# Column halves throughout the second expert layer, and earlier combine weights, in an attention and soft mixture-of-experts kernel

## The chip, the cores and the metric

The kernel runs on one core of a Trainium2 chip. The metric is the device time of one execution in microseconds (us). The core's engines are written as in the profile: PE is TensorE (its matmuls; PEld its weight loads), DVE is VectorE, ACT is ScalarE, POOL is GpSimd, SP is SyncE, which here issues every data transfer. Each engine works through its own queue in order.

## The reference

Attention with 32 pooled keys per head comes first, and its output, 4608 rows of 512, goes into a soft mixture of 8 experts with 4 slots each:

```python
logits = x @ phi                                   # 4608 x 32
d = exp(logits - logits.max(0)); d /= d.sum(0)     # over the rows
slot_input = (d.T @ x).reshape(8, 4, 512)
for e in range(8):
    h = maximum(slot_input[e] @ w1[e], 0)          # 4 x 1024
    slot_out[e] = h @ w2[e]                        # 4 x 512
c = exp(logits - logits.max(1)); c /= c.sum(1)     # over the slots
out = c @ slot_out.reshape(32, 512)                # 4608 x 512
```

Everything is float32. `w1` and `w2` are 16 MB each, the output is 9.4 MB.

## The kernel before, in words

**Stages.** The batches are taken in four pairs: keys and values are pooled, scores and softmax formed, logits made, and each pair's share of the slot inputs summed. The shares are joined into `SIM` (line 1000), the slot inputs of all experts, which holds each expert's 4 slots in columns of their own and zeros beside them. Then three things follow. The first layer (`expert_in`, line 1097) multiplies `SIM` with `w1`, two tiles of 1 MB per expert; `hidden` (lines 1113, 1122 and 1128) applies the rectifier and transposes the result into `hT`, four experts at a time. The second layer (`expert_out`, line 1148) multiplies `hT` with `w2`, again two tiles of 1 MB per expert, 16 in all. The output stage (`out_mult`, line 1280) multiplies the combine weights `cT` with the slot outputs `sr`, 36 row blocks of 128 x 512, copies each from a PSUM bank to SBUF on ACT or DVE and writes it out.

**The second layer.** One tile of `w2` takes four matmuls of 32 columns of weights each, which stand side by side in the array and write the four quarters of the 128 partitions. All tiles of all experts add into one accumulator, since the unused rows of `hT` are zero. So at the end the accumulator holds, in each quarter of the partitions, a part of the sum for all 32 slots; a matmul with `rep` (line 1080), a matrix of four stacked identities repeated, adds the four quarters and repeats the result. The accumulator `pacc` is the PSUM tile `kvbank`, two banks of 512 floats. Before the change the first 15 tiles add 512 columns wide into bank 0. The last tile (expert 7, second half) comes in four transfers of 256 KB, two for each half of the columns, and its products are made apart: the first column half goes to bank 1, the second to the first half of bank 0.

**`slot_sums` (lines 1070, 1075 and 1080).** It copies an accumulator from PSUM to SBUF, the first column half on DVE and the second on ACT, and multiplies it with `rep` into `scbank`, one bank for each half. It is called twice: `slot_sums(0)` for the first 15 tiles, ahead of the last tile's products, and `slot_sums(1)` for the last tile; the two matmuls for a half add up in `scbank`. After it, line 1266 on ACT rounds each half of the sum to `sr` and line 1271 on DVE stores the rounding's remainder beside it; the output matmuls use both (two matmuls per block).

**Combine weights.** `slots(bp)` makes `cT` for one of the four pairs: about nine DVE instructions of 0.2 to 0.5 us (lines 1198 to 1220), one exponential on ACT, five transposes on PE into two banks (line 1231) and three copies on ACT (lines 1240 to 1244). Before the change it stands behind every second expert of the second layer.

**Fills.** `fill` adds matmuls of ones into an unused half bank of `kvbank` (line 476) that nothing reads. Two stand behind the 15th `w2` tile.

**What sets the order.** Each piece of work is handed to a planner (`add`) with its engine, an estimated cost and what it reads and writes. The planner picks, step by step, the piece that can start first by its own clock (ties by the order of the program) and so fixes the order in each engine's queue before anything runs; the costs and the place in the program move work only that way. The waits between engines are put in afterwards by the framework, from the tiles that are read and written. It takes `kvbank` and `scbank` as wholes: an access to one bank waits for the other engines' earlier accesses to the other bank.

**The end.** The first output tile of three row blocks is written in three transfers of 256 KB (line 1313) so that it can start early; its six half blocks are copied at lines 1302 (ACT) and 1304 (DVE), alternating. The other 33 blocks go in 11 transfers of 768 KB (line 1343), with copies at lines 1333 (ACT) and 1335 (DVE).

## Time and profile before

| | |
|---|---|
| Time, median of three runs | 216.18 us (216.16 to 221.99) |
| Profiled execution, its own time | 219.04 us |
| Its span, first to last instruction | 217.2 us |
| Busy in the span | PE 175.2, PEld 108.8, DVE 131.7, ACT 70.0, POOL 86.6 us |
| Moved by DMA | 76.45 MB, mean 352 GB/s |
| Granted PE clock, mean | 0.918 |

A row of the timeline gives start, length, engine, line, operation and form, the count, and in brackets how long the engine had been idle and for what. A float32 matmul stands in the trace as two records, so the four matmuls of a `w2` tile are "x8". The chain of waits follows the work that ended last back to the start, each piece to what released it; "issue" in it is time in which the engine waited for nothing that the profile shows. In a table of stretches each engine has its busy time and, in brackets, its instructions; then come the granted PE clock as a fraction, the busy share of the 16 DMA engines, and what they moved.

### The profile page before, as it was taken

Reading aid. Unit: us, or ns where it says so; the run is one execution under the profiler, and the core shown is the slowest. Engines: PE = TensorE matmul, PEld = TensorE weight load, DVE = VectorE, ACT = ScalarE, POOL = GpSimd, SP = SyncE. Lnnn points to the kernel's source line nnn. Section 1 sums busy time; section 2 is a strip of 40 time slices with the busy share of each in tenths; the row PEclk is TensorE's granted clock in tenths of the full one; section 3 lists DMA queues with packets and bytes.
Section 4 is the critical chain, followed back from the end, with each engine's and each line's share of the span. In section 5 each row is a group of like instructions: output and inputs, shape, how many; then the busy total and the mean of one; then the engine's idle time right before and its main releaser. Section 6 shows DMA issues by size and latency. Waiting matters only on the chain.

```text
span 217.2 us, 5728 instructions
## 1 busy us (share of the span) xinstructions
PE 175.2 (81%) x2462; PEld 108.8 (50%) x2462; DVE 131.7 (61%) x226; ACT 70.0 (32%) x186; POOL 86.6 (40%) x85
## 2 busy tenths in 40 slices
PE   8798977696598997969889799777999995899600
PEld 6576754465474574455565368543553331366200
DVE  6835047969539999967964995459300750189600
ACT  2042234443423726134742332020100321267500
POOL 6298009697952795399932484200000000000000
PEclk9999999859579999799997999996999999999955
DMA  6999999999999999999889979499999995059997
GB/s 214 386 392 391 380 393 375 390 381 392 385 388 389 385 408 347 393 391 388 322 293 414 367 269 400 118 410 345 409 404 410 408 407 195 5 199 416 414 413 295
DMA packets 28985, 76.45 MB, mean 352 GB/s; under 512 B 1824, under 2 KB 6944, under 8 KB 28960
## 3 DMA queue, kind: packets, MB, share of 16 engines
q1 hardware_dynamic: 28960, 76.09, 92.8%
q8 instruction: 19, 0.31, 0.6%
q14 instruction: 6, 0.05, 0.1%
HBM read 66.65 MB, written 9.44 MB: 350 GB/s over the span
## 4 chain that ended last, share of the span: by engine, by line
PE 40%; DMA 22%; DVE 13%; POOL 9%; issue 6%; ACT 3%; SPq 1%; DVEq 1%; POOLq 0%; ACTq 0%
DMA top<-in_q_dram 10%; DMA arena<-in_moe_w_dram 9%; PE kvbank L476 7%; PE bank L1097 6%; PE bank L785 5%; PE scbank L716 5%; PE kvbank L599 4%; PE bank L1280 3%; DMA out_dram<-arena 3%; DVE arena L700 3%; POOL arena L562 3%; POOL arena L774 3%; PE bank L849 2%; POOL arena L751 2%; DVE arena L511 2%
## 5 line engine op out<-in xcount | busy, mean ns | idle before, releaser
L549 POOL TENSOR_TENSOR arena<-arena 128x1152 f32<-128x1152 f32 x8 | 21.0, 2631 | 17.4 <-ACT arena L544 14.7
L476 PE MATMUL kvbank<-ones 128*128 128x256 f32 x96 | 26.2, 411 | 2.2 <-ACT arena L622 1.1
L700 DVE STREAM_TRANSPOSE arena<-top 128x1152 f32<-128x1152 f32 x16 | 21.7, 1358 | 7.0 <-DMA top<-in_q_dram 7.0
L716 PE MATMUL scbank<-arena 64*64 64x288 f32 x256 | 22.5, 447 | 3.0 <-DVE arena L730 2.5
L774 POOL TENSOR_TENSOR arena<-arena,ssm 128x576 f32<-128x576 f32 x16 | 18.4, 1158 | 15.6 <-DVE ssm L770 15.6
L562 POOL TENSOR_TENSOR arena<-arena 128x128 f32<-128x128 f32 (+2 forms) x32 | 23.4, 730 | 2.3 <-ACT arena L555 0.3
L599 PE MATMUL kvbank<-arena 64*32 64x128 f32 x1152 | 20.7, 278 | 4.3 <-ACT arena L555 2.7
L785 PE MATMUL bank<-arena 128*128 128x288 f32 x64 | 21.8, 475 | 2.0 <-DVE arena L777 2.0
L751 POOL TENSOR_TENSOR arena<-arena,smx 128x576 f32<-128x576 f32 x16 | 18.4, 1158 | 12.3 <-DVE smx L746 12.3
L476 PEld LDWEIGHTS kvbank<-ones 128*128 128x128 f32 x96 | 18.2, 202 | 7.7 <-issue 2.5
L599 PEld LDWEIGHTS kvbank<-arena 64*32 64x32 f32 x1152 | 16.5, 107 | 8.4 <-issue 3.8
L511 DVE TENSOR_REDUCE arena<-arena 128x128 f32<-128x1152 f32 x8 | 17.1, 2143 | 5.1 <-DMA arena<-in_phi_dram 5.1
L1148 PE MATMUL kvbank<-arena 128*32 128x512 f32 (+1 forms) x136 | 15.6, 573 | 3.8 <-DMA arena<-in_moe_w_dram 2.6
L730 DVE STREAM_TRANSPOSE arena<-scbank 128x576 f32<-128x576 f32 x16 | 12.2, 764 | 9.2 <-PE scbank L716 9.1
L785 PEld LDWEIGHTS bank<-arena 128*128 128x128 f32 x64 | 12.7, 215 | 7.5 <-DVE arena L777 3.0
L777 DVE STREAM_TRANSPOSE arena<-arena 128x576 f32<-128x576 f32 x16 | 12.2, 760 | 5.2 <-POOL arena L774 5.0
L1097 PE MATMUL bank<-arena,SIM 128*32 128x256 f32 x224 | 13.9, 409 | 1.7 <-DVE SIM L1000 1.7
L1280 PE MATMUL bank<-sr,cT 64*128 64x512 f32 (+1 forms) x78 | 14.6, 417 | 0.4 <-DVE sr L1271 0.2
L716 PEld LDWEIGHTS scbank<-arena 64*64 64x64 f32 x256 | 9.3, 139 | 11.1 <-DVE arena L730 4.1
L756 ACT ACTIVATE arena<-arena 128x576 f32<-128x576 f32 x16 | 11.0, 686 | 8.7 <-POOL arena L751 8.6
L1335 DVE COPY arena<-bank 128x512 f32<-128x512 f32 x17 | 11.5, 690 | 2.6 <-DMA out_dram<-arena 1.6
L1280 PEld LDWEIGHTS bank<-sr,cT 64*128 64x128 f32 x78 | 9.3, 184 | 5.7 <-DVE arena L1335 3.2
(111 smaller groups left out, 233.7 us busy)
## 6 DMA issues: line engine op xcount, KB each, us to landing
arena<-in_moe_w_dram SPq DMA_DIRECT2D x29, 1024.0 KB, 9.1
top<-in_q_dram SPq DMA_DIRECT2D x8, 1152.0 KB, 13.6
arena<-in_k_dram SPq DMA_DIRECT2D x8, 1152.0 KB, 10.7
arena<-in_v_dram SPq DMA_DIRECT2D x8, 1152.0 KB, 13.2
out_dram<-arena SPq DMA_DIRECT2D x11, 768.0 KB, 7.6
arena<-in_phi_dram SPq DMA_DIRECT2D x8, 576.0 KB, 8.2
top<-in_moe_w_dram SPq DMA_DIRECT2D x2, 1024.0 KB, 7.1
arena<-in_moe_w_dram SPq DMA_DIRECT2D x4, 256.0 KB, 15.4
```

The costliest lines, as they stand in the source:

```text
L476: lambda: nc.tensor.matmul(warm.ap, ones, ones.unsqueeze(1).to_broadcast([P, 2, P]), start=True, stop=True,),
L511: lambda: nc.vector.tensor_reduce(mx.ap, ph().rearrange("p c j m -> p c m j"), axis=AX.X, op=ALU.max),
L549: lambda: nc.gpsimd.tensor_tensor(ph(), ph(), mb.ap.unsqueeze(2).to_broadcast([P, C, J, M]), op=ALU.subtract),
L562: plus = lambda o, x, y: nc.gpsimd.tensor_tensor(o, x, y, op=ALU.add)
L599: nc.tensor.matmul(acc.ap[M * c: M * c + M, a, : 2 * D], ph()[h0: h0 + HALF, c, j, :], kv()[h0: h0 + HALF, :, c, j * D: j * D + D], start= ...
L700: nc.vector.transpose(qT.ap.rearrange("p (i u y) -> p u i y", i=2, y=Y), qt.ap[:, h * QT_SZ: h * QT_SZ + QT_SZ].rearrange("p (u i x) -> p ...
L716: nc.tensor.matmul(scb.ap[HALF * g: HALF * g + HALF, a, :JY], kb[g].ap[h0: h0 + HALF, i, c].rearrange("p r m -> p (r m)"), qT[g][c // 2].a ...
L751: lambda: nc.gpsimd.tensor_tensor(exv(), exv(), bc(mx), op=ALU.subtract),
L774: lambda: nc.gpsimd.tensor_tensor(exv(), exv(), bc(sm), op=ALU.mult),
L785: nc.tensor.matmul(lp.ap[:, :JY], vpb.ap[:, h, :], aT.ap[:, a * JY: (a + 1) * JY], start=(h == 0), stop=(h == H - 1),)
L1097: nc.tensor.matmul(hb.ap[NS * j: NS * j + NS, :256], SIM.ap[:, 2 * i + c, NS * e: NS * e + NS], wv[:, c, 256 * j: 256 * j + 256], start=(e ...
L1280: nc.tensor.matmul(po.ap[:, : x.stop - x.start], cT[bp].ap()[y: y + HALF, j // 2 * P: j // 2 * P + P], sr.ap[y: y + HALF, t, x], start=(t ...
```

## The change

The second layer adds 256 columns at a time into the two banks for all 16 tiles: column half d into bank d, from the first tile to the last. The last tile's products join the same sums, so `slot_sums` is called once, at the end, and makes one copy and one `rep` matmul for each half instead of two. The second copy buffer (`acs`) goes. The two fills behind the 15th tile go. `slots` stands behind each of the first four experts. Of the six half-block copies of the first output tile, all three of the first column half are now on ACT; before, one of them (i = 1) was on DVE. Transfers, their sizes and their order stay.

```diff
-    hTs, acs = over([8 * E * (NS + SE)], 1), over([DM], 2)
+    hTs, acs = over([8 * E * (NS + SE)], 1), over([DM], 1)
...
-    accs = [acs.tile().split(2) for _ in range(2)]
+    accs = acs.tile().split(2)
...
-    def slot_sums(x):
+    def slot_sums():
         for d in range(2):
...
+            x = slice(d * HD, d * HD + HD)
+            add(
+                *((ACT, act(HD)) if d else (DVE, dve(HD))),
+                lambda d=d, x=x: (nc.scalar.copy if d else nc.vector.tensor_copy)(
+                    accs.ap[:, x], pacc.ap[:, d, :HD]
+                ),
+                r=[pacc.part(d)], w=[accs.part(d)],
+            )
             add(
                 PE, 0.5,
-                lambda d=d, dst=dst: nc.tensor.matmul(
-                    so[d].ap, rep.rearrange("p a n -> p (a n)"), dst(),
-                    start=(x == 0), stop=(x == 1),
+                lambda d=d, x=x: nc.tensor.matmul(
+                    so[d].ap, rep.rearrange("p a n -> p (a n)"), accs.ap[:, x],
+                    start=True, stop=True,
                 ),
-                r=[accs[x].part(d), rep_b], w=[so[d]],
+                r=[accs.part(d), rep_b], w=[so[d]],
             )
...
-                add(
-                    PE, 0.9,
-                    lambda mult=mult, i=i: mult(
-                        pacc.ap[:, 0], 0, DM, e == 0 and i == 0, e == E - 1
-                    ),
-                    r=[hTb.part(e // EG), t], w=[pacc.part(0)],
-                )
-                if e == E - 1:
-                    fill(2, FILL + 7, [t])
+                for d in range(2):
+                    add(
+                        PE, 0.5,
+                        lambda d=d, mult=mult, i=i: mult(
+                            pacc.ap[:, d], d * HD, HD, e == 0 and i == 0, False
+                        ),
+                        r=[hTb.part(e // EG), t], w=[pacc.part(d)],
+                    )
                 continue
...
-            slot_sums(0)
             for d in range(2):
                 add(
-                    PE, 0.5, lambda d=d, mult=mult: mult(pacc.ap[:, 1 - d], d * HD, HD, True, True),
-                    r=[hTb.part(e // EG), t.part(2 * d), t.part(2 * d + 1)], w=[pacc.part(1 - d)],
+                    PE, 0.5, lambda d=d, mult=mult: mult(pacc.ap[:, d], d * HD, HD, False, True),
+                    r=[hTb.part(e // EG), t.part(2 * d), t.part(2 * d + 1)], w=[pacc.part(d)],
                 )
...
-        if e % 2 == 1:
-            slots(e // 2)
-    slot_sums(1)
+        if e < NBP:
+            slots(e)
+    slot_sums()
...
-                if i % 2 == d:
+                if d == 0 or i == 1:
                     nc.scalar.copy(dst, po.ap[:, :HD])
```

Lines below the edit have moved up by 5 to 8: the second layer's matmul is line 1142 in the changed kernel, the copies are 1068, the `rep` matmul 1075, the transposes of `slots` 1223, the two pieces of `sr` 1258 and 1263, the output matmul 1272.

The order of the queues changes in three places. The first is PE's queue at the end of the second layer, from the last part of the 15th tile on. DMAHW0 to DMAHW3 are the landings of the last tile's four transfers, in order, the first two for the first column half. A count is of matmuls; a row with a wait waits for the engines named. Before:

```order
L1148 MATMUL kvbank<-arena 32x512 x3
L476 MATMUL kvbank<-ones 128x256
L1148 MATMUL kvbank<-arena 32x256 [waits DMAHW0_49,Activation_49]
L1148 MATMUL kvbank<-arena 32x256 [waits DMAHW1_49]
L1148 MATMUL kvbank<-arena 32x256 x2
L1080 MATMUL scbank<-arena,rep 128x256 x2
L1148 MATMUL kvbank<-arena 32x256 [waits DMAHW2_49,DVE_49]
L1148 MATMUL kvbank<-arena 32x256 [waits DMAHW3_49]
L1148 MATMUL kvbank<-arena 32x256 x2
L1080 MATMUL scbank<-arena,rep 128x256
L476 MATMUL kvbank<-ones 128x256 [waits Activation_49]
L1080 MATMUL scbank<-arena,rep 128x256 [waits Activation_49]
```

With the change:

```order
L1142 MATMUL kvbank<-arena 32x256 x7
L1142 MATMUL kvbank<-arena 32x256 [waits DMAHW0_49]
L1142 MATMUL kvbank<-arena 32x256 [waits DMAHW1_49]
L1142 MATMUL kvbank<-arena 32x256 x2
L1075 MATMUL scbank<-arena,rep 128x256 [waits DVE_49]
L1142 MATMUL kvbank<-arena 32x256 [waits DMAHW2_49]
L1142 MATMUL kvbank<-arena 32x256 [waits DMAHW3_49]
L1142 MATMUL kvbank<-arena 32x256 x2
L1075 MATMUL scbank<-arena,rep 128x256 [waits DVE_49,Activation_49]
```

The fills and the two first `rep` matmuls are gone; the last tile's first half waits for its landings alone, no longer for a copy on ACT; the `rep` matmul of the first half stands ahead of the last tile's second half and waits for the copy on DVE.

The second place is ACT's queue at the same time, where `kvbank` is copied (1075, now 1068), `sr` rounded (1266, now 1258) and the first half blocks are copied (1302, now 1294). Before:

```order
L1075 COPY arena<-kvbank 128x256 [waits DVE_49,Activation_49]
L1075 COPY arena<-kvbank 128x256 [waits DVE_49,PE_49]
L1266 CAST sr<-scbank 128x256 [waits PE_49]
L1266 CAST sr<-scbank 128x256 [waits DVE_49]
L1302 COPY arena<-bank_65 128x256 [waits DMAHW0_49,PE_49]
L1302 COPY arena<-bank_63 128x256 [waits PE_49]
L1302 COPY arena<-bank_65 128x256 [waits PE_49]
```

With the change:

```order
L1258 CAST sr<-scbank 128x256 [waits PE_49]
L1068 COPY arena<-kvbank 128x256 [waits DVE_49,PE_49,Activation_49]
L1258 CAST sr<-scbank 128x256 [waits PE_49]
L1294 COPY arena<-bank_65 128x256 [waits DMAHW0_49,PE_49]
L1294 COPY arena<-bank_62 128x256 [waits PE_49]
L1294 COPY arena<-bank_63 128x256 [waits PE_49]
L1294 COPY arena<-bank_65 128x256 [waits PE_49]
```

One copy of `kvbank` is gone, the other stands between the two roundings, and a fourth half-block copy has come.

The third place is PE's queue in the second layer, where the transposes of `slots` stand between the tiles (four matmuls a tile before, eight with the change). Before:

```order
L1148 MATMUL kvbank<-arena 32x512 x12
L1231 MATMUL bank_63<-ident,arena 128x128 x3
L1231 MATMUL bank_64<-ident,arena 128x128
L1231 MATMUL bank_64<-ident,arena 64x128
L1148 MATMUL kvbank<-arena 32x512 x16
L1231 MATMUL bank_62<-ident,arena 128x128 x3
L1231 MATMUL bank_63<-ident,arena 128x128
L1231 MATMUL bank_63<-ident,arena 64x128
L1148 MATMUL kvbank<-arena 32x512 x16
L1231 MATMUL bank_64<-ident,arena 128x128 x3
L1231 MATMUL bank_62<-ident,arena 128x128
L1231 MATMUL bank_62<-ident,arena 64x128
```

With the change:

```order
L1142 MATMUL kvbank<-arena 32x256 x8
L1223 MATMUL bank_63<-ident,arena 128x128 x3
L1223 MATMUL bank_64<-ident,arena 128x128
L1223 MATMUL bank_64<-ident,arena 64x128
L1142 MATMUL kvbank<-arena 32x256 x16
L1223 MATMUL bank_62<-ident,arena 128x128 x3
L1223 MATMUL bank_63<-ident,arena 128x128
L1223 MATMUL bank_63<-ident,arena 64x128
L1142 MATMUL kvbank<-arena 32x256 x20
L1223 MATMUL bank_64<-ident,arena 128x128 x3
L1223 MATMUL bank_62<-ident,arena 128x128
L1223 MATMUL bank_62<-ident,arena 64x128
```

The four sets of transposes stood behind tiles 4, 8, 12 and 13; they stand behind tiles 2 and 4, in the middle of tile 7, and in the middle of tile 10. The queue of SP is the same, and that of DVE too, up to the copies of the end.

More of the change, by code (lines that the diff above doesn't have):

```diff
@@ L1058 @@
     HD = DM // 2
-    accs = [acs.tile().split(2) for _ in range(2)]
+    accs = acs.tile().split(2)
     sr = keep("sr", [P, 2, DM], dtype=F32R, parts=2)
     so = [Tile(ap=scbank[:, d, :HD]) for d in range(2)]
-    def slot_sums(x):
+    def slot_sums():
         for d in range(2):
-            cols = slice(d * HD, d * HD + HD)
-            src = lambda d=d, cols=cols: pacc.ap[:, 0, cols] if x == 0 else pacc.ap[:, 1 - d, :HD]
-            dst = lambda cols=cols: accs[x].ap[:, cols]
-            if d == 0:
-                add(
-                    DVE, dve(HD), lambda src=src, dst=dst: nc.vector.tensor_copy(dst(), src()),
-                    r=[pacc.part(0) if x == 0 else pacc.part(1 - d)], w=[accs[x].part(d)],
-                )
-            else:
-                add(
-                    ACT, act(HD), lambda src=src, dst=dst: nc.scalar.copy(dst(), src()),
-                    r=[pacc.part(0) if x == 0 else pacc.part(1 - d)], w=[accs[x].part(d)],
-                )
+            x = slice(d * HD, d * HD + HD)
[6 more added lines that the diff above has]
+            )
             add(
                 PE, 0.5,
-                lambda d=d, dst=dst: nc.tensor.matmul(
-                    so[d].ap, rep.rearrange("p a n -> p (a n)"), dst(),
-                    start=(x == 0), stop=(x == 1),
+                lambda d=d, x=x: nc.tensor.matmul(
+                    so[d].ap, rep.rearrange("p a n -> p (a n)"), accs.ap[:, x],
+                    start=True, stop=True,
                 ),
-                r=[accs[x].part(d), rep_b], w=[so[d]],
+                r=[accs.part(d), rep_b], w=[so[d]],
             )
@@ L1161, in expert_out @@
                 )
-                add(
-                    PE, 0.9,
-                    lambda mult=mult, i=i: mult(
-                        pacc.ap[:, 0], 0, DM, e == 0 and i == 0, e == E - 1
-                    ),
-                    r=[hTb.part(e // EG), t], w=[pacc.part(0)],
-                )
-                if e == E - 1:
-                    fill(2, FILL + 7, [t])
+                for d in range(2):
[6 more added lines that the diff above has]
+                    )
                 continue
@@ L1306 @@
             add(
-                *((ACT, act(HD)) if i % 2 == d else (DVE, dve(HD))), f,
+                *((ACT, act(HD)) if d == 0 or i == 1 else (DVE, dve(HD))), f,
                 r=[po], w=[ot0.part(2 * i + d)],
```

## Prediction

> **What bounds the kernel now.** I read the page's slices first, to see where the transfers stop.
>
> ```profile
> GB/s 214 386 392 391 380 393 375 390 381 392 385 388 389 385 408 347 393 391 388 322 293 414 367 269 400 118 410 345 409 404 410 408 407 195 5 199 416 414 413 295
> ```
>
> Each slice is 5.43 us. Nearly everywhere the core moves about 400 GB/s; at the end come 195, 5 and 199, and then the outputs at 414. So there is a hole late in the program, between the last weights and the first output. A table of stretches shows its edges.
>
> ```profile
> core 0: us, PE busy (x) PEld busy (x) DVE busy (x) ACT busy (x) POOL busy (x), PEclk, DMA share, GB/s
> 144.10:147.50 3.40, 1.58 (x17) 1.23 (x16) 2.06 (x7) 0.18 (x1) 0.00 (x0) 1.00 0.98 386
> 148.10:151.00 2.90, 2.86 (x28) 1.38 (x32) 2.61 (x8) 0.44 (x1) 0.00 (x0) 0.51 0.92 369
> 151.00:154.00 3.00, 3.00 (x60) 1.68 (x56) 2.77 (x8) 0.44 (x1) 0.00 (x0) 1.00 1.06 416
> 163.80:177.20 13.40, 13.39 (x119) 4.38 (x109) 6.09 (x16) 3.05 (x10) 0.00 (x0) 1.00 1.02 408
> ...
> 181.70:185.10 3.40, 1.70 (x10) 0.45 (x10) 0.42 (x1) 0.00 (x0) 0.00 (x0) 1.00 0.16 53
> 185.30:191.90 6.60, 6.06 (x41) 3.26 (x41) 2.07 (x6) 2.33 (x7) 0.00 (x0) 1.00 0.01 4
> 196.00:202.00 6.00, 6.00 (x33) 4.21 (x32) 5.45 (x8) 4.47 (x9) 0.00 (x0) 1.00 1.02 417
> ```
>
> From 185.3 to 191.9 the DMA share is 0.01, and from 196 on it is full. What the outputs need is fixed, so the kernel ends a fixed time after the first output is issued. Whatever shortens the chain across this hole shortens the kernel one for one; work that is saved while transfers run full saves nothing. The chain of waits through the hole:
>
> ```profile
> 162.28 20.28 DMA arena<-in_moe_w_dram
> 182.60 1.06 PE kvbank L1148 x8
> 183.67 0.64 PE kvbank L476 x2
> ...
> 184.34 0.44 DVE arena L1070
> ...
> 184.81 0.32 issue
> 185.13 0.38 ACT arena L1075
> 185.51 0.04 issue
> 185.55 0.64 PE kvbank L1148 x8
> 186.19 1.06 PE scbank L1080 x4
> 187.25 0.57 PE kvbank L1148 x8
> ...
> 188.45 0.56 PE kvbank L476 x2
> 189.01 0.61 PE scbank L1080 x2
> ...
> 190.11 0.38 ACT sr L1266
> ...
> 190.51 0.44 DVE sr L1271
> ...
> 190.99 6.98 PE bank L1280 x35
> ```
>
> The 15th tile, transferred since 162.28, lands at 182.56. Then everything is serial: its products, a fill, the copy of the first half on DVE, that of the second on ACT, and only then the last tile's first half on PE, at 185.55. That is late against its data. Of the two transfers for this half the later one was issued at 165.7 and took 18.2 us, so it landed at 183.9. The last transfer of all was issued at 174.5 and took 10.7 us, so it landed at 185.2.
>
> ```profile
> L458 SPq DMA_DIRECT2D arena<-in_moe_w_dram x1: 6299/6299/6299, 165.7 to 165.7; - x1
> DMA to landing us min/median/max: 18.2/18.2/18.2
> ```
>
> ```profile
> L458 SPq DMA_DIRECT2D arena<-in_moe_w_dram x1: 2317/2317/2317, 174.5 to 174.5; - x1
> DMA to landing us min/median/max: 10.7/10.7/10.7
> ```
>
> So at the start of the hole the kernel waits for its copies and not for its data: 185.55 less 183.9 is 1.6 us. The second column half of `sr` is ready at 190.95, 5.7 us after the last landing.
>
> **The change, part by part.** First the hole, step by step, with the profiled durations: the chain's, and these rows of PE's and of ACT's timeline. A step that follows another engine's starts 0.04 us after it (the piece at 185.51 of the chain).
>
> ```profile
> 182.60 1.06 PE L1148 MATMUL kvbank<-arena 128*32 128x512 f32 x8 [1.50 <-DMA arena<-in_moe_w_dram]
> ...
> 185.55 0.64 PE L1148 MATMUL kvbank<-arena 128*32 128x256 f32 x8 [1.25 <-ACT arena L1075]
> ...
> 187.18 0.64 PE L1148 MATMUL kvbank<-arena 128*32 128x256 f32 x8
> 188.91 0.70 PE L1080 MATMUL scbank<-arena,rep 128*128 128x256 f32 x2
> ```
>
> ```profile
> 185.13 0.37 ACT L1075 COPY arena<-kvbank 128x256 f32<-128x256 f32 x1 [5.26 <-DVE arena L1070]
> 187.89 0.37 ACT L1075 COPY arena<-kvbank 128x256 f32<-128x256 f32 x1 [2.39 <-PE kvbank L1148]
> ```
>
> - 15th tile, now two times four narrow matmuls. As one block it takes 1.06 (first row of the chain behind the landing). I keep 1.06: 182.60 to 183.7. The narrow form is priced below.
> - First half of the last tile: no fill, no copy ahead of it, only the landing at 183.9. From 184.0, 0.64: 184.6.
> - Copy on DVE, 0.44 with the step to PE: to 185.1. `rep` matmul, once, 0.70: 185.1 to 185.8.
> - Second half of the last tile stands behind it in PE's queue. Its data is there since 185.2, so the queue costs it some 0.5. The next group starts 0.07 before the one ahead has ended (187.18 against 187.25): 185.75 to 186.4.
> - Copy of this half on ACT: 0.37. The rounding of the first half (185.85 to 186.2) is ahead of it in the queue and is done. Start 0.07 after PE (as 187.82 to 187.89): 186.45 to 186.85.
> - `rep` matmul of the second half, 0.70: 186.9 to 187.55. Rounding on ACT, 0.37, to 187.95. Remainder on DVE, 0.44, to 188.4. First output matmuls that need it: 188.45.
>
> Before, these output matmuls started at 190.99. The gain is 2.54. One price is open: at 184.81 ACT stood 0.32 us in "issue" behind a wait before it copied, and the copy at 187.89 did not. With the hole on ACT the gain is 2.2, without it 2.5. I take 2.4, nearer to the second, because the copy now follows another ACT instruction closely, where at 187.89 it had been idle for 2.39 without a hole, and at 185.13 ACT had been idle for 5.26 us.
>
> The first output transfers, on SP's queue:
>
> ```profile
> 191.90 1.34 SPq L1313 DMA_DIRECT2D out_dram<-arena  x3
> ```
>
> From the output matmuls to the first output transfer it took 0.91 us (190.99 to 191.90). I leave that. The half-block copy that moves from DVE to ACT is one of 0.37 there, behind a rounding that ends at 187.95; three overlapped copies end by 189.3 or so, before the matmul of the next half block gives ACT work. DVE is relieved at a place where it waited for PE anyway. Bounds: 0.1 either way.
>
> Now the work ahead of the hole: narrow matmuls, and `slots` earlier.
>
> ```profile
> 157.78 4.52 PE L1097 MATMUL bank<-arena,SIM 128*32 128x256 f32 x80
> 168.59 3.64 PE L1148 MATMUL kvbank<-arena 128*32 128x512 f32 x32
> 176.43 0.76 PE L1231 MATMUL bank<-ident,arena 128*128 128x128 f32 x5
> 177.49 1.06 PE L1148 MATMUL kvbank<-arena 128*32 128x512 f32 x8 [0.30 <-DMA arena<-in_moe_w_dram]
> ```
>
> A wide tile, 8 records, costs 0.91 us in a stream (3.64 for 32). The first layer has the narrow form, 32 columns of weights and 256 moving ones: 80 records in 4.52, so 16 in 0.90. Nearest row, so I price the narrow tile at the wide one, +0. The upper end is two isolated halves, 2 x 0.64 = 1.28, +0.36. What covers it: PE was through tile 12 and three sets of transposes at 177.19 and waited for weights from there. With the fourth set ahead (0.7) it would be at 177.9, and three more tiles without waiting end at 180.7. They are needed by 183.9. So 3.2 us are free over 15 tiles, 0.21 a tile; up to there the narrow form and the earlier `slots` cost nothing. Beyond, every 0.01 a tile costs 0.15, and at 0.37 a tile (a tile of 1.30) the gain is gone. `slots` also needs DVE and ACT between two sets of transposes; they were busy for 6.09 and 3.05 of the 13.40 us from 163.8 to 177.2, and where a set has to wait for them after all, the same 3.2 us cover it. The transfers of weights wait for buffers that the first layer frees, not for the second.
>
> [...]
>
> The sum: profiled execution 219.04 (span 217.2, 1.84 around it) less 2.4 is 216.6, span 214.8. The median of the runs is 216.18, 2.86 under the profiled execution. I see nothing in the hole that the profiling stretches, and take the same gain from the median: **213.8 us**.
>
> **The rivals.** The weight loads of the second layer in this part of the program, by count, shortest, median and longest:
>
> ```profile
> L1148 PEld LDWEIGHTS kvbank<-arena x40: 106/108/109, 177.5 to 187.2; 128*32 128x32 f32 x40
> ```
>
> First, **the weight loads become the bound**: two times as many per tile, at 0.106 us each. If they don't overlap, a tile takes 16 x 0.106 = 1.70, 0.77 more than now; 15 x (0.77 - 0.21) = 8.4 lost, net 6.0 slower: 222.2. It decides from 1.30 a tile. Against it: in 151 to 154 the first layer's 56 weight loads of this form kept PEld busy for 1.68 of 3.00 us while 60 matmuls passed, so they run beside each other. Chance 0.04. [...]
>
> Second, **the clock**. The fills keep PE busy where it waits. In 148.1 to 151 the granted clock was 0.51 and 28 records passed in 2.86 us, against 60 in 3.00 at 1.00; ahead of it lay a stretch with PE busy for 1.58 of 3.40. Without the fills such a stretch could come just ahead of the hole. If the clock then halves inside it, the four PE groups of the sum (0.64, 0.70, 0.64, 0.70) at most double: 2.7 lost, 216.5; with the fixed part of each group unchanged, about 1.7 lost, 215.5. Against it: 181.7 to 185.1 had PE busy for 1.70, the fill's 0.64 among them, and the clock stayed; in its place now stands the first half of the last tile, 0.64 too. Chance 0.10. [...]
>
> Third, **new waits on ACT and in the signals**. ACT now rounds, copies and rounds in one queue. With 0.32 of "issue" at each of its three steps 1.0 is lost. And a wait can be released by a later instruction than the one it needs: the copy at 184.34 waited for the fill, though its data was ready at 183.66. If the first rounding is released only by the second half's products, 186.4 instead of 185.85, 0.4 more is lost. Together the gain falls from 2.5 to about 1.1: 215.1. Chance 0.10.
>
> **How the numbers follow.** The forecast has 0.76. Its own range is 213.3 to 214.2: the ACT hole, the copies, and some tenths in the landings. Down to 212.8 I allow for a landing earlier than profiled; upward the range takes in the third rival and the likelier half of the second, to 215.9. A difference of 2% (4.3 us) is about what a measurement of this kernel can tell from no change; the gain is 1.1%. Slower by more than that needs the first rival at its full price, or a clock that falls in several places: 0.04. Faster by more needs almost the whole hole to vanish, or fewer halved stretches earlier on: 0.04. Within: 0.92.
>
> **What would show it.** In the changed profile: the narrow tiles at 0.9 us in a stream, and PE waiting for weights from the 13th tile on; the last tile's first half starting at its landing; the first output transfer 4.1 to 4.5 us behind the last weight landing, where it was 6.6; outputs then at 415 GB/s to the end, in the same 24 to 25 us. The forecast is wrong if PE does not wait for weights any more, if the clock is under 1.00 between the last landing and the first output, or if the output transfers have gaps.

## The result, and the profile after

The changed kernel takes 215.22 us, median of 7 runs (213.66 to 218.73), against 217.04 for the kernel before in the same comparison (7 runs, 216.16 to 221.99). Some executions are longer, those of the changed kernel at a lower granted clock (217.63 and 218.73 us at 0.904, against 213.66 to 215.84 at 0.923 to 0.932); these medians hold them too, the ratio leaves them out. The ratio is 0.989, 95% interval 0.985 to 0.993. So the changed kernel is 1.1% faster: less than the 2% that the prediction named as telling, but the interval does not contain 1. Of 217.04 us that is 2.4 us, with an interval of 1.6 to 3.3.

The profiled execution of the changed kernel has a span of 216.9 us (218.73 with what lies around it), hardly less than the 217.2 before. It happened to run at half clock for a longer stretch ahead of the hole than the one before, and its last weights landed 1.6 us later; so the two spans can't be set against each other, but what follows the last landing can. The page's slices:

```profile
GB/s 210 383 393 390 379 393 376 390 380 394 385 386 390 385 405 349 390 393 377 348 270 411 410 349 309 130 321 206 372 418 408 407 409 384 55 209 410 415 417 292
```

Where 195, 5 and 199 stood there is now 384, 55 and 209: the hole is still there, but it fills less than a slice. The slices 321 and 206 ahead of it, where 410 and 345 stood, lie in the stretch at half clock. The table of stretches:

```profile
core 0: us, PE busy (x) PEld busy (x) DVE busy (x) ACT busy (x) POOL busy (x), PEclk, DMA share, GB/s
141.30:154.90 13.60, 11.15 (x100) 6.58 (x88) 8.10 (x22) 2.10 (x8) 0.00 (x0) 0.50 0.78 287
...
186.83:191.07 4.24, 3.63 (x27) 2.20 (x27) 1.34 (x4) 2.41 (x7) 0.00 (x0) 1.00 0.00 0
195.00:203.00 8.00, 7.69 (x40) 4.28 (x38) 6.41 (x11) 5.00 (x10) 0.00 (x0) 1.00 1.01 412
```

For 13.6 us from 141.3 on the clock was 0.50, where the execution before had some 3.4 us of it there. The middle row is the hole: its edges are the landing of the last transfer of weights, by this view of its issues (the last at 176.0, landed 10.8 later; the one before the two last at 168.8, landed 16.7 later, at 185.5),

```profile
L458 SPq DMA_DIRECT2D arena<-in_moe_w_dram x3: 2317/2334/4718, 168.8 to 176.0; - x3
...
DMA to landing us min/median/max: 10.8/12.6/16.7
```

and the first output issue in SP's timeline:

```profile
191.07 2.05 SPq L1305 DMA_DIRECT2D out_dram<-arena  x3
```

186.83 to 191.07 are 4.24 us, where 185.25 to 191.90 were 6.65. In it the clock is 1.00 and nothing is transferred. The chain of waits through it:

```profile
164.78 19.34 DMA arena<-in_moe_w_dram
184.12 0.04 issue
184.16 2.06 PE kvbank L1142 x24
186.23 0.02 issue
186.25 0.44 DVE arena L1068
186.69 0.04 issue
186.73 0.70 PE scbank L1075 x2
187.43 0.61 PE kvbank L1142 x8
188.04 0.03 ACTq L1068
188.07 0.04 issue
188.11 0.38 ACT arena L1068
188.49 0.04 issue
188.54 0.71 PE scbank L1075 x2
189.25 0.02 issue
189.27 0.38 ACT sr L1258
189.65 0.02 issue
189.68 0.43 DVE sr L1263
190.11 0.04 issue
190.16 2.10 PE bank L1272 x13
```

The 24 records at 184.16 are the 15th tile (16) and the last tile's first half (8). The half needs the landing at 185.52 and is through at 186.23, 0.71 later, so it starts at its data. From that landing to the output matmul at 190.16 it takes 4.64 us. The fills and the copy ahead of the last tile are gone from the chain; the second half (187.43) stands behind the `rep` matmul of the first, though its data is there since 186.83.

The narrow tiles in PE's timeline:

```profile
169.91 1.93 PE L1142 MATMUL kvbank<-arena 128*32 128x256 f32 x32
...
178.89 4.09 PE L1142 MATMUL kvbank<-arena 128*32 128x256 f32 x72
184.16 2.03 PE L1142 MATMUL kvbank<-arena 128*32 128x256 f32 x24 [1.18 <-DMA arena<-in_moe_w_dram]
```

16 records make a tile: 0.965 us between transposes, 0.91 in the stream (4.09 for 72), as the wide one. PE waits for weights before the 15th tile only.

One thing got worse. The end comes 25.8 us behind the first output issue, where it was 25.3. The three first transfers took these times to land (before: 2.1/2.3/2.5), and in the 1.1 us from 191.2 the DMA queues carried, beside them, a fetch of instructions:

```profile
DMA to landing us min/median/max: 2.3/2.7/2.9
```

```profile
q1 hardware_dynamic: 64, 0.13, 32.0%
q8 instruction: 1, 0.02, 5.8%
```

5.8% of 16 engines over 1.1 us are one DMA engine for 1.0 us, with a transfer of 16 KB. In the execution before such a fetch fell to 187.79, into the empty hole. So the hole shrank by 2.41 us, but the stretch from the last landing to the end by 1.9 only (31.95 to 30.07).

### The profile page after: what moved, and what is told of

It is laid out like the page before. It is cut to its first block, busy times and chain, and to the rows that moved or that the text cites. A ratio compares the mean times of both kernels' runs of the same rounds, so it can differ in the third digit from the quotient of the medians.

```text
span 216.9 us, 5947 instructions
## 1 busy us (share of the span) xinstructions
PE 176.8 (81%) x2574; PEld 112.3 (52%) x2574; DVE 130.6 (60%) x224; ACT 70.0 (32%) x186; POOL 86.6 (40%) x85
## 4 chain that ended last, share of the span: by engine, by line
PE 45%; DMA 22%; DVE 14%; POOL 6%; issue 4%; ACT 3%; SPq 1%; DVEq 1%; ACTq 0%; POOLq 0%
DMA top<-in_q_dram 10%; DMA arena<-in_moe_w_dram 9%; PE bank L1091 7%; PE kvbank L476 6%; PE bank L785 6%; PE scbank L716 6%; PE kvbank L599 5%; PE bank L849 3%; DMA out_dram<-arena 3%; DVE arena L700 3%; PE bank L1272 3%; DVE arena L730 2%; DVE arena L511 2%; PE bank L875 2%; POOL arena L549 2%
## 5 line engine op out<-in xcount | busy, mean ns | idle before, releaser
L476 PE MATMUL kvbank<-ones 128*128 128x256 f32 x92 | 25.4, 420 | 2.2 <-ACT arena L622 1.1
L774 POOL TENSOR_TENSOR arena<-arena,ssm 128x576 f32<-128x576 f32 x16 | 18.4, 1158 | 16.7 <-DVE ssm L770 16.7
L716 PE MATMUL scbank<-arena 64*64 64x288 f32 x256 | 21.7, 433 | 3.0 <-DVE arena L730 2.5
L599 PE MATMUL kvbank<-arena 64*32 64x128 f32 x1152 | 21.5, 285 | 1.8 <-issue 1.1
L599 PEld LDWEIGHTS kvbank<-arena 64*32 64x32 f32 x1152 | 17.1, 110 | 6.0 <-issue 3.8
L1142 PE MATMUL kvbank<-arena 128*32 128x256 f32 x256 | 16.0, 382 | 1.2 <-DMA arena<-in_moe_w_dram 1.2
L1091 PE MATMUL bank<-arena,SIM 128*32 128x256 f32 x224 | 14.8, 429 | 1.2 <-DVE SIM L1000 1.2
L716 PEld LDWEIGHTS scbank<-arena 64*64 64x64 f32 x256 | 9.0, 137 | 10.8 <-DVE arena L730 4.5
L761 DVE TENSOR_REDUCE ssm<-arena 128x18 f32<-128x576 f32 x16 | 11.5, 722 | 2.0 <-ACT arena L756 2.0
## 6 DMA issues: line engine op xcount, KB each, us to landing
top<-in_q_dram SPq DMA_DIRECT2D x8, 1152.0 KB, 13.6
```

The source lines that it names most:

```text
L476: lambda: nc.tensor.matmul(warm.ap, ones, ones.unsqueeze(1).to_broadcast([P, 2, P]), start=True, stop=True,),
L599: nc.tensor.matmul(acc.ap[M * c: M * c + M, a, : 2 * D], ph()[h0: h0 + HALF, c, j, :], kv()[h0: h0 + HALF, :, c, j * D: j * D + D], start= ...
L716: nc.tensor.matmul(scb.ap[HALF * g: HALF * g + HALF, a, :JY], kb[g].ap[h0: h0 + HALF, i, c].rearrange("p r m -> p (r m)"), qT[g][c // 2].a ...
L774: lambda: nc.gpsimd.tensor_tensor(exv(), exv(), bc(sm), op=ALU.mult),
L1091: nc.tensor.matmul(hb.ap[NS * j: NS * j + NS, :256], SIM.ap[:, 2 * i + c, NS * e: NS * e + NS], wv[:, c, 256 * j: 256 * j + 256], start=(e ...
```

## The experiments

All twelve kernels were timed in 6 to 12 runs beside runs of the kernel before; the ratio is to that kernel. The other columns, in us, come from each kernel's profiled execution: the hole is the time from the last landing of weights to the first output issue; "first" is the first output transfer from issue to landing; "rest" the time from the first output issue to the end of the span; "tail" is hole and rest together. A span is read to 0.1 us, and so are "rest" and "tail". The first output transfer has 256 KB, in the three kernels with half writes 128 KB. The two kernels of this study stand first.

| kernel | ratio, 95% | hole | first | rest | tail |
|---|---|---|---|---|---|
| before | 1 | 6.65 | 2.1 | 25.3 | 31.95 |
| changed | 0.989 (0.985 to 0.993) | 4.24 | 2.7 | 25.8 | 30.07 |
| changed, again | 0.989 (0.978 to 0.999) | 4.24 | 2.6 | 25.8 | 30.0 |
| before without fills | 0.997 (0.992 to 1.001) | 6.00 | 2.1 | 25.4 | 31.4 |
| six fills | 1.003 (0.998 to 1.008) | 6.80 | 2.1 | 25.4 | 32.2 |
| slots back | 0.994 (0.989 to 0.999) | 4.22 | 2.9 | 26.1 | 30.35 |
| spread behind | 0.991 (0.987 to 0.994) | 4.83 | 2.8 | 26.0 | 30.85 |
| own bank | 0.990 (0.986 to 0.994) | 4.13 | 3.1 | 25.9 | 30.0 |
| fetch early | 0.987 (0.981 to 0.993) | 4.26 | 2.1 | 25.3 | 29.6 |
| quarter columns | 1.012 (1.006 to 1.018) | 7.56 | 2.1 | 26.6 | 34.1 |
| copies back | 0.996 (0.991 to 1.000) | 4.64 | 2.9 | 26.1 | 30.7 |
| half writes | 0.993 (0.989 to 0.998) | 3.24 | 4.0 | 27.1 | 30.4 |
| half writes, fetch early | 0.991 (0.986 to 0.995) | 3.25 | 1.9 | 26.5 | 29.8 |
| all three | 0.987 (0.982 to 0.993) | 3.05 | 1.8 | 26.2 | 29.3 |

The theory that is tested: the kernel's time follows the tail, one for one; the hole's chain makes up the gain, and what lies under full transfers costs nothing. The rivals: the gain comes from elsewhere (the earlier `slots`, the fills alone), or narrow matmuls cost.

**The changed kernel again.**

> The changed kernel once more, as the measure for the others. I call the stretch from the last weight landing to the issue of the first output transfer the hole: 6.65 us in the profile before, 4.24 in the profile after. My theory: the time follows the hole. Hole 4.2 +- 0.2 us, time 2.4 us (1.1%) under before. If instead the first profile was a chance and the gain lies ahead of the hole, the hole will come out nearer to 6.6 while the time is still lower.

The hole is 4.24 in this execution too, though the last landing came at 184.38 here and at 186.83 there. The hole is a property of the program; where it lies is one of the execution.

**The fills alone.** The kernel before, without these two lines:

```diff
-                if e == E - 1:
-                    fill(2, FILL + 7, [t])
```

> The kernel before, with only the two fills taken out. My theory: the first fill (0.64 us) stands between the 15th tile and the copy on DVE, so the hole shrinks by 0.6, to 6.0 us; the second ends before a wait for ACT that is due anyway and gives nothing. Time about 0.6 us (0.3%) under before. A rival has the fills carry the whole gain: then the hole is 4.2 and the time 2.4 us lower. Another has the fills hold the clock up: then the granted clock falls under 1.00 between the last landing and the first output, and the time is no lower.

The hole is 6.00: of the 2.41 us the fills are 0.65. In the time, 0.997, so small a step can't be told from none. The last tile's first half still waits for ACT's copy:

```profile
182.07 0.64 PE L1148 MATMUL kvbank<-arena 128*32 128x256 f32 x8 [1.30 <-ACT arena L1075]
```

**A cost put back.** The changed kernel with six matmuls of ones between the 15th tile and the last one's first half (a scratch part of PSUM takes their result):

```diff
+            late = Tile(ap=scbank[:, 1, 256:512])
+            for _ in range(6):
+                add(PE, WC, lambda: nc.tensor.matmul(late.ap, ones, ...),
+                    r=[ones_b, pacc], w=[late])
...
-                    r=[hTb.part(e // EG), t.part(2 * d), t.part(2 * d + 1)], w=[pacc.part(d)],
+                    r=[hTb.part(e // EG), t.part(2 * d), t.part(2 * d + 1), late], w=[pacc.part(d)],
```

> The changed kernel with six matmuls of ones, into a bank that nothing uses then, between the 15th tile and the first half of the last one. They cost 6 x 0.43 + 0.27 = 2.9 us on PE, of which some 0.3 lies in the wait for the landing. If the time follows the hole one for one: hole 6.7 us, time 2.5 us over the changed kernel, so the same as before to within 0.3%. If the outputs' stage takes up such a delay, the time stays nearer to the changed kernel's than to that of before.

```profile
185.68 2.86 PE L1176 MATMUL scbank<-ones 128*128 128x256 f32 x12
188.47 1.07 PE L1142 MATMUL kvbank<-arena 128*32 128x256 f32 x16
```

With 2.86 us of PE put ahead of the last tile's halves the hole is 2.56 longer, and the gain is gone: 1.003 against 0.989. Not all of the 2.56 is the matmuls' own: in this kernel the `rep` matmuls stand behind both halves, an order that by itself takes 0.59 ("spread behind", below). Narrow products and the earlier `slots` are in this kernel as well, and it gains nothing. So the gain is made in the hole.

**`slots` back to where it was.**

```diff
-        if e < NBP:
-            slots(e)
+        if e % 2 == 1:
+            slots(e // 2)
```

> The changed kernel with the combine weights behind every second expert again, as before. My theory: the earlier place of that work gives nothing, since PE has some 3 us of room ahead of the last landings: hole 4.2 +- 0.2 us, time as the changed kernel's. The rival, that the gain comes from these transposes leaving the end of the second layer: hole larger by 0.7 us (one set of transposes) and time up by as much.

The hole is the same, 4.22. The ratio, 0.994, lies above the changed kernel's 0.989, but the intervals overlap. As its tail is 0.3 us longer (the fetch, below) and the landings scatter by more than that, whether `slots` is worth anything ahead of the hole is not settled.

**The middle block's copy back on DVE.** The last part of the change undone alone:

```diff
-                if d == 0 or i == 1:
+                if i % 2 == d:
```

> The changed kernel with the first output tile's copies dealt to the two engines as before the change (the middle block's first half to VectorE again). Theory 1 (the copy was moved beside the path: it is done before the second half's output matmul starts, whichever engine makes it): hole 4.2 us within 0.1, time within 0.3% of the changed kernel. Theory 2 (it helped, by keeping VectorE free for the second half's remainder): hole 4.5 to 4.6 us, since the remainder would stand up to 0.43 us behind the copy.

The second theory held: the hole is 4.64. DVE's and PE's timelines:

```profile
185.38 0.42 DVE L1296 COPY arena<-bank 128x256 f32<-128x256 f32 x1 [1.46 <-PE bank L1272]
185.73 0.41 DVE L1263 TENSOR_TENSOR sr<-scbank,sr 128x256 fp32r<-128x256 f32 x1
```

```profile
186.20 0.96 PE L1272 MATMUL bank<-sr,cT 64*128 64x256 f32 x7 [0.48 <-DVE sr L1263]
```

ACT's rounding had ended at 185.28 (184.91 and 0.37), but the remainder starts at 185.73, behind the copy. The copy's move to ACT is worth 0.4 us of the hole. With 0.65 for the fills and 0.40 for this, 1.36 of the 2.41 are left for the halves themselves, if the parts add up; the halves were not undone by themselves.

**Narrower still.** The first 15 tiles in pieces of 128 columns:

```diff
-                        lambda d=d, mult=mult, i=i: mult(
-                            pacc.ap[:, d], d * HD, HD, e == 0 and i == 0, False
-                        ),
+                        lambda d=d, mult=mult, i=i: [
+                            mult(pacc.ap[:, d, y: y + HD // 2], d * HD + y, HD // 2,
+                                 e == 0 and i == 0 and y == 0, False)
+                            for y in (0, HD // 2)
+                        ],
```

> The changed kernel with the second layer's matmuls of the first 15 experts cut once more, 128 columns each: 32 matmuls (two records each as before would be 32 x 2 per expert against 16) for the same products. Theory 1 (with 32 columns of weights, four at a time beside each other, a matmul costs by its columns only): still 0.9 to 1.0 us for an expert, hole 4.2 us, time within 0.3% of the changed kernel. Theory 2 (a matmul has a least time of some 0.057 us per record at this shape, that of 256 columns, set by its weight load or its issue): 1.8 us for an expert, 27 us for 15 experts and 4 us of transposes from 167 us on, so that TensorE ends some 10 us after the weights: time 8 to 12 us (4 to 5%) above the changed kernel, and no wait for weights.

The expectation says expert where it means a tile. Neither theory had the outcome, though the first had the price. The rows of PE's timeline, and its waits by cause from 165 to 190 us:

```profile
174.40 2.26 PE L1142 MATMUL kvbank<-arena 128*32 128x128 f32 x73
178.29 0.86 PE L1142 MATMUL kvbank<-arena 128*32 128x128 f32 x23 [1.63 <-issue]
...
179.78 3.02 PE L1142 MATMUL kvbank<-arena 128*32 128x128 f32 x99
184.86 2.81 PE L1142 MATMUL kvbank<-arena 128*32 128x128 f32 x85 [2.05 <-issue]
```

```profile
PE kvbank L1142 <- issue: 3.8, 3, 2.1
```

The price by columns held: 32 records are a tile now, and 99 in 3.02 make 0.98 a tile, as with half the records of twice the width. Nearly as many weight loads go with the records (158 beside 166 from 169.53 to 175.73), and they set no floor above that 0.98. Yet PE stood still three times, 3.8 us in all (0.16, 1.63 and 2.05), with nothing it waited for, and the hole grew to 7.56. In the trace a fetch of 16 KB starts ahead of each stop: at 169.53, 175.73 and 182.33, each 1.1 us long; and PE goes on 1.4 to 1.5 us after each has ended (172.08, 178.29, 184.86). The author's reading is that in these stops PE had run out of instructions. It rests on the times alone, three stops of three, and was not shown by a run of its own; the next fetch, at 185.98, is followed by no stop.

**The fetch under the first output.** Six 128-column matmuls of ones where PE is ahead of its data, behind the 10th tile (the second of expert 4, counted from 0; the expectations here and below say the 13th expert). They move the next fetch (at 191.24 in the changed kernel, 0.17 behind the first output issue) and change no order:

```diff
+    late = Tile(ap=scbank[:, 1, 256:384])
...
+        if e == E - 4:
+            for _ in range(6):
+                add(PE, 0.0, lambda: nc.tensor.matmul(late.ap, ones, ones, start=True, stop=True),
+                    r=[ones_b, pacc], w=[late])
```

> The changed kernel with six 128-column matmuls of ones into a free part of PSUM behind the products of the 13th expert, where TensorE is ahead of the weight loads. They change nothing in the order of the rest; they only move the point in TensorE's instruction stream at which the next 16 KB of instructions are fetched by some 12 records, from the first output transfer (191.24 us in the changed kernel, the transfer issued at 191.07) back ahead of the first output issue. Theory 1 (the fetch, one transfer of 1.0 us on one DMA engine, holds up the first output transfer): the first output transfer takes 2.1 us from issue to landing as before the change, not 2.6 to 2.7; from the first output issue to the span's end 25.3 us as in the kernel before, not 25.8; hole 4.2 us; time 0.5 us (0.25%) below the changed kernel. Theory 2 (it is the first output transfer's place that makes it slow, not the fetch): 2.6 to 2.7 us to landing and 25.8 us to the end as in the changed kernel, wherever the fetch falls.

The first theory held in each number of the profile: the fetch lies at 185.64, 1.51 ahead of the first output issue (187.15), the first three output transfers take what they took before the change, and the rest is 25.3.

```profile
DMA to landing us min/median/max: 2.1/2.3/2.5
```

```profile
187.15 1.33 SPq L1316 DMA_DIRECT2D out_dram<-arena  x3
```

The three issues also take 1.33 on SP again, where they took 2.05. The table bears it out over all kernels: the first transfer takes 2.6 to 4.0 us in the seven in which a fetch started between 0.1 and 2 us behind the first issue, and 1.8 to 2.1 in the seven in which none did. (In one of these, "half writes, fetch early", the fetch had started 0.64 before the first issue and ran on for 0.71 behind it; the transfer took 1.9 against 1.8.) In time, 0.987 against 0.989, it can't be told.

**The order of the halves.** The `rep` matmuls behind both halves' products:

```diff
-                r=[accs.part(d), rep_b], w=[so[d]],
+                r=[accs.part(d), rep_b, pacc.part(1)], w=[so[d]],
```

> The changed kernel, with one more read on the matmuls that spread a half's sum over the partitions: they also wait for the second half's products, so that the queue of TensorE runs both halves' products first and then both of these matmuls. Theory 1 (the two spread sums lie in one tile of PSUM, and the waits are kept for that tile as a whole): the queue saves the 0.5 us that the second half stood behind the first spread matmul, but ScalarE's rounding of the second half now also waits until VectorE has read the first half's sum; from the end of the second half's products to the output matmul it is the 3.14 us of the run with six fills, where the two stood in this order too. Hole from the last landing to the first output issue 4.6 to 4.7 us against 4.24, time 0.4 us (0.2%) above the changed kernel. Theory 2 (waits are kept for each half apart): the 0.5 us of queue are simply saved, hole 3.7 to 3.8 us, time 0.5 us below the changed kernel.

The first theory held, and by more: 4.83. The waits that it named are in DVE's and ACT's timelines:

```profile
185.76 0.42 DVE L1263 TENSOR_TENSOR sr<-scbank,sr 128x256 fp32r<-128x256 f32 x1 [2.64 <-PE scbank L1075]
186.62 0.42 DVE L1263 TENSOR_TENSOR sr<-scbank,sr 128x256 fp32r<-128x256 f32 x1 [0.44 <-ACT sr L1258]
```

```profile
186.21 0.37 ACT L1258 CAST sr<-scbank 128x256 fp32r<-128x256 f32 x1 [1.25 <-DVE sr L1263]
```

The first half was rounded at 184.97, but its remainder waits for PE's `rep` matmul of the other half (185.73), and ACT's second rounding waits for DVE's first remainder. Both halves of `scbank` are one tile to the framework, and its waits are kept for the tile. What lies above the expected 4.6 to 4.7 has another cause: the copy of the second half on ACT starts 0.38 us behind PE's products (184.31 after 183.93), where it is 0.11 in the changed kernel. Without that the hole would be some 4.56, an estimate from these rows. Besides, the granted clock fell to 0.50 at 187.26, in the last 0.8 us of this hole, the only hole of the fourteen in which it did. So the order that the change has, with the second half behind the first `rep` matmul, is the better one of the two by some 0.3 us, though it costs 0.5 us of queue; the times, 0.991 and 0.989, don't tell them apart.

**Two tiles for the two sums.** The same, and the second half's sum in a bank of its own:

```diff
-    so = [Tile(ap=scbank[:, d, :HD]) for d in range(2)]
+    so = [Tile(ap=scbank[:, 0]), b_l.tile()]
```

> The kernel with the spread matmuls behind both halves' products, and the second half's spread sum in a tile and bank of its own. Theory 1 (the hole's chain is what counts, and the shared tile is what made the order of the halves cost): second half's products start at the last landing, 0.56 us; copy 0.38, spread matmul 0.65 to 0.7, rounding 0.38, remainder 0.43, output matmul 2.8 us behind the last landing (3.3 in the changed kernel): hole 3.7 to 3.85 us against 4.24, time 0.45 us (0.2%) below the changed kernel. Theory 2 (VectorE or ScalarE is full between the halves, so the order doesn't matter): hole stays 4.2 us.

The hole is 4.13: 0.7 below the run before, but 0.1 below the changed kernel instead of 0.45. PE's timeline and the chain say why:

```profile
183.65 0.74 PE L1142 MATMUL kvbank<-arena 128*32 128x256 f32 x8 [0.54 <-DVE arena L1068]
```

```profile
184.43 0.03 ACTq L1068
184.46 0.32 issue
184.78 0.38 ACT arena L1068
```

`kvbank` is one tile too, so the second half's products wait for DVE's copy of the first half (here only until its data came anyway); and ACT lost 0.32 in "issue" ahead of its copy, where the changed kernel loses 0.04. Without the 0.28 the hole would be some 3.85, the upper end of what the first theory gave. What these late copies go with is told below, under the hole on ACT.

**The first tile in six writes.** One transfer for each half block, behind its copy:

```diff
-            if d == 1:
-                add(SP, 0.06, lambda i=i: nc.sync.dma_start(
-                        outv[:P, i, :], ot0.ap[:, i * DM: i * DM + DM]), ...)
+            add(SP, 0.06, lambda i=i, d=d, x=x: nc.sync.dma_start(
+                    outv[:P, i, x], ot0.ap[:, i * DM + d * HD: i * DM + d * HD + HD]), ...)
```

> The changed kernel with the first output tile written in six transfers of 128 KB, one behind each half block's copy, in place of three of 256 KB. The first half's three copies end at 190.1 us, 1.0 us ahead of the first output issue of the changed kernel. Theory 1 (whatever starts the output stream earlier counts): hole 3.2 to 3.3 us against 4.24. The fetch of instructions at 191.24 then meets transfers that run already; from the first issue to the end 25.8 to 26.3 us; time 0.5 us (0.2%) below the changed kernel, 1.0 at most. Theory 2 (six issues and shorter rows cost what the start brings, or the output blocks behind them are not ready in time): the stream is as long as it starts earlier, time as the changed kernel's.

> The six half writes and the fetch of instructions moved ahead of them (the six 128-column matmuls of ones behind the 13th expert). Theory 1 (both gains stand by themselves): hole 3.2 to 3.3 us, from the first issue to the end 25.3 to 25.8 us, from the last landing to the end 28.5 to 29.1 us against 30.0 of the changed kernel; time 1.0 us (0.5%) below the changed kernel. Theory 2 (as for the half writes alone: issues or rows give it back): from the last landing to the end 29.5 us, as with the fetch moved alone.

> Half writes, the fetch moved, and the second half's spread sum in a bank of its own behind both halves' products. The bank alone brought 0.11 us of hole. Theory 1 (the terms add): from the last landing to the end 28.4 to 29.0 us, time 1.1 us (0.5%) below the changed kernel. Theory 2 (the bank taken for the sum is missed by the first output blocks, of which one more must then wait for a bank): hole 0.3 us or more above that of the run before.

The hole fell by 1.0 as computed, and the tail hardly at all: 30.4 and 29.8, where the kernels without half writes have 30.0 and 29.6. SP's timelines of the three:

```profile
188.18 3.67 SPq L1304 DMA_DIRECT2D out_dram<-arena  x6
```

```profile
191.48 3.03 SPq L1315 DMA_DIRECT2D out_dram<-arena  x6
```

```profile
186.97 2.81 SPq L1315 DMA_DIRECT2D out_dram<-arena  x6
```

In the third, whose fetch had ended before the first issue, the six issues still take SP 2.81 us, some 0.5 each, for 768 KB, which at the 412 GB/s that the changed kernel moves from 195 to 203 take 1.9. So the 1.0 us is given back: the second theory. Its two reasons can't be parted, for the next tile's copies end hardly earlier than the issues (in the second kernel at 194.18, the issues at 194.51). In the third kernel both theories miss: its hole is 3.05, 0.2 under the second's, and the tail 29.3, the shortest of all. It and the kernel with the fetch moved have the lowest ratio, 0.987, but their intervals contain the changed kernel's 0.989; no version is shown to beat it.

## Why the prediction was right, point by point

- **The bound.** Right. A straight line through the fourteen rows of the table gives 1.1 us of time for each us of tail (an estimate from the table), and a cost put into the hole came back as time (six fills). That "the kernel ends a fixed time after the first output is issued" held only to 0.5 us here; over all kernels the rest is 25.3 to 27.1. The prediction's own sum was against the profiled execution: 2.4 us; measured are 2.41 in the hole and 2.4 (1.6 to 3.3) in the time. That both agree to the tenth is luck: the tail shrank by 1.9, which the interval of the time holds as well. The 213.8 stands below the measured 215.22 since it was taken from 216.18, the median of three runs, where seven in the comparison have 217.04. So 215.22 lies in the upper part of the range, which was meant for two rivals, and neither of them came.
- **The chain.** Right, step by step. From the landing of the first half's data to the output matmul the prediction had 4.55 (183.9 to 188.45); it took 4.64. The half starts at its landing; the second half loses 0.5 in the queue; the step from the output matmul to the first issue is 0.91 still.
- **The hole on ACT.** The prediction left 0.32 open and leaned to no hole, since the copy follows another ACT instruction closely. None came in the changed kernel, but the reason is not borne out: there the first rounding starts 0.04 behind its matmul after 7.89 us of idle time, and in "before without fills" a copy after only 2.52 had the hole. The trace has something that goes with it. In six of the fourteen (before, before without fills, six fills, spread behind, own bank, all three) ACT's first copy of `kvbank` starts 0.37 to 0.38 us behind what it waits for, and in each of them the last 8 KB transfer of the second instruction queue (q14) starts 0.63 to 0.67 behind the copy's start (before: 185.78 after 185.13). In the other eight the copy starts 0.11 behind, and that transfer lies at 167 to 173 (changed: 171.42), well ahead of the hole. So in all fourteen traces the late start goes with the place of an instruction fetch, and the changed kernel may be without it only because of where its fetch falls. Nothing was run to move that fetch alone, so the cause is argued and not shown.
- **Narrow tiles at +0.** Right within 0.05 a tile (0.91 to 0.965), and the price still goes by columns in the quarter columns (0.98). That PE would wait for weights from the 13th tile on was wrong: it waited for the 15th alone, 1.18 us, and 1.15 in the repetition. The cover of 3.2 us was taken from an execution with the first layer done at 163.84; in the two of the changed kernel the second layer started at 166.87 and 164.58. The cover was enough, but thinner than the text says. One reading there is off: by the waits of SP in the profile before, one weight transfer was held for 3.0 us by a set of transposes of `slots` (3.8 with the change), so not all buffers are freed by the first layer. It cost nothing that can be seen, since the last transfers land 0.6 to 0.8 apart in both profiles. In the price of the first rival 1.70 less 0.91 is 0.79 and not 0.77, which moves its 222.2 by 0.3.
- **The copy that moved, ±0.1.** The one mis-sized step inside the hole. "DVE is relieved at a place where it waited for PE anyway": with the shorter chain, it would have copied just when the second rounding ended, 0.4 late for the remainder. The sum was not touched, since its chain let the remainder follow the rounding at once, which the move makes true.
- **The outputs "in the same 24 to 25 us"**: not the same. From the first issue to the last landing they took 24.3 us before and 24.9 after, 0.5 more, for the fetch of instructions (with it moved, "fetch early", the rest is the 25.3 of before again), which the prediction did not look at. "415 GB/s" held (410, 415 and 417 in the slices).
- **The rivals.** Weight loads: refuted by the quarter columns, 0.98 a tile with twice the loads of the changed kernel. The clock: 1.00 in the hole, with PE busy for 3.63 of 4.24; that it can fall there without the fills shows in "spread behind" (0.50 from 187.26). New waits: the rounding of the first half was not held up by the second's products in the changed kernel; the waits by whole tiles that this rival spoke of are real, and decide as soon as the order is another (spread behind).

## What to carry to other kernels

Look for the stretch in which no transfer runs, follow the chain across it, and count only what is on it. Under full transfers the same microseconds need not count: the 1.60 us of ones in "fetch early" left the hole at 4.26. Before reordering by halves, ask for which whole tile the framework keeps its waits, and which engine's free moment the shorter chain needs: a copy that cost nothing beside the long chain (before, the remainder starts 0.02 behind ACT's rounding) cost 0.40 us beside the short one ("copies back", 4.64 against 4.24). Cutting these matmuls in two was cheap by columns (0.91 us a tile at 512, 0.91 to 0.965 at 256, 0.98 at 128), but it doubles their instructions, which have to be fetched too: 19 fetches before, 20 with halves, 22 with quarters.

## What the hardware showed that was not expected

- The instruction queue q8 fetches 16 KB at a time, each as one transfer of 0.9 to 1.4 us, 19 to 22 in an execution. One under the first output transfer lengthened the rest by 0.4 to 0.8 us (25.8 to 26.1 in six kernels with whole writes, against 25.3 to 25.4 in four without one there). Quarter columns has none there either, but one at 196.09, under later outputs, and a rest of 26.6; why it is so long no run shows.
- With 128-column matmuls under full transfers PE stood still for 1.63 and 2.05 us beside such fetches.
- The same program's last landing lay at 184.38 in one execution and 186.83 in another, with 6.8 and 13.6 us at half clock between 141 and 155 us, while the hole was 4.24 in both. The two spans differ by 2.5 us and the two last landings by 2.45, so in these two executions the difference was made ahead of the hole.
